# A row transform of 512 points as four products of 128 columns, with first-layer weights loaded in rearranged quarters

## The chip, the cores and the metric

One core of one Trainium2 chip runs the kernel. Its engines work side by side: TensorE (PE) multiplies matrices, VectorE (DVE) and ScalarE (ACT) work element by element, GpSimd (POOL) does small work and issues DMAs, SyncE (SP) only issues DMAs. The time is that of one execution on the device in microseconds (us); the median of several runs is what counts.

## The reference

The input x has 2048 rows of 512 numbers, in bf16. Each row is normalized (xn), and three terms are added:

```python
xn = _layernorm(x, axis=-1)
return x + _A_ref(xn, A_w_r, A_w_i) + _B_ref(xn, B_w_gate, B_w_up, B_w_down)

def _A_ref(x, w_r, w_i):       # S = 2048, D = 512, weights [2048, 257]
    X = rfft2(x.astype(float32), axes=(-2, -1))
    return irfft2(X * (w_r + 1j * w_i), s=(S, D)).astype(bfloat16)

def _B_ref(x, w_gate, w_up, w_down):    # 512 -> 1792 -> 512
    g, u = x @ w_gate, x @ w_up
    return (gelu(g) * u) @ w_down
```

So there is a two-dimensional Fourier filter over all rows (A) and a gated feed-forward layer (B), both on the same normalized rows.

## The kernel before

**Tiles.** The 2048 rows are 16 tiles j of 128 rows; four tiles make a block m. For each tile DVE takes statistics (`ln_stat`, `ln_aggr`; for tiles 0 and 1 `ln_first`, with ACT's square root), GpSimd raises the variance to the power -1/2 (L683, all tiles but 0 and 1), and `ln_norm` writes the normalized row in one operation of 512 columns, on DVE (12 tiles) or ACT (4). `trans` turns the tile with four PE transpositions (it needs the identity, `ident`), and DVE or ACT copy the result from PSUM to `xnT[m]`: four chunks `dc` of 128 of the 512 columns on the partitions, 512 rows along the free axis.

**Feed-forward.** `gate_up` (L990) multiplies weight chunks with `xnT`, for each block and each of 14 blocks `fc` of 128 hidden columns. The first four `fc` of block 0 are done in two parts, tiles 0 and 1 first, then 2 and 3. Blocks 2 and 3 use a scheme with seven products (`gate_up7`, L1074). `down` (L1168) is the second layer, also with seven products; its last product in the last block is `last_prod` (L1183), two halves of 256 columns in two PSUM banks, each followed by an add on DVE (L1188); two output DMAs wait for both adds.

**Filter.** `butter` folds the 512 columns of a block: chunks 0, 1 plus and minus chunks 2, 3 (two operations of 1024 columns, L740 and L741), and the sum once more (two of 512, L742 and L743). `unit_D` (L754 to L757) is the transform along a row, 16 units: the frequencies divisible by 4 and those 2 off that have one product of 128 columns each, while the odd ones have two products of 256 columns over 2 x 128 rows of weights. ACT brings the result to `xs`. Then come `unit_A` and a trip through DRAM (`scr1`, back into `tv`), `unit_B`, the filter, `unit_C`, a second trip, `unit_E` and `unit_F`. `unit_B` needs all eight pieces of `tv`.

**Loads.** Each of the two weight matrices of the first layer is loaded in five pieces by `load_w`: ten DMAs on SP, each over all 128 partitions and all four chunks `dc`, 256 KB for two `fc`. x comes in halves of 64 partitions, the first ones by SP and ACT; the row transform's constants `fd` in one DMA of 192 KB.

**Order.** A list scheduler (`_Plan`) runs while the kernel is built. It gives every instruction a fixed place in its engine's queue, by assumed durations and a priority for each of 1026 tasks, written out in `ORDER`; `GATES` holds some late DMAs and DVE steps back until PE has come to a given priority. [...] SP's start list before is 26 DMAs; GpSimd's queue begins with two memsets, then the powers of tiles 2 and 3, then those of later blocks and the late DMAs (L670: the second layer's weights, the filter's weights `W`, constants).

Of the kernel before, what the change touches and what calls it, by code (L numbers as in the profile page):

```python
# [29 lines left out]
def _constants():  # L30
# [9 lines left out]
    m64 = np.arange(64)[None, :]  # L40
    a0 = tp * (p + 0.5) * (4 * m64) / D
    a2 = tp * (p + 0.5) * (4 * m64 + 2) / D
    im0 = -np.sin(a0)
    im0[:, 0] = (-1.0) ** np.arange(P)
    fo = []
    for c in range(2):
        kodd = np.concatenate([4 * m64[0] + 1, 4 * m64[0] + 3])[None, :]
        a = tp * (p + P * c + 0.5) * kodd / D
        fo += [np.cos(a), -np.sin(a)]
    FD = np.concatenate([np.cos(a0), im0, np.cos(a2), -np.sin(a2)] + fo, 1)  # L50
# [426 lines left out]
def bass_parallel_sum__spectral_gfnet__glu_gated_geglu__prompt_kernel(  # L477
# [25 lines left out]
    with ExitStack() as es:  # L503
# [103 lines left out]
        def act(fn, n, r, w, prio, over=(), **kw):  # L607
            return add("act", fn, r=r, w=w, over=over, occ=n / 1200 + 0.055, lat=n / 1200 + 0.24, prio=prio, **kw)
# [13 lines left out]
        def wkey(nm, fs, dcs=(0, 1)):  # L622
            return [("w" + nm, f, i) for f in fs for i in dcs]
# [821 lines left out]
```

## Time and profile before

| | us |
|---|---|
| runs shown | 176.8, 178.35, 178.53; median 178.35 |
| profiled execution | 176.34 |
| its span (first to last instruction) | 174.5 |
| PE, DVE, ACT, POOL busy | 169.8, 150.4, 118.4, 51.2 |
| mean granted clock of PE | 0.999 |

Busy time is the union of an engine's instructions, and matmuls overlap: one of 256 columns is shown with 0.273 us, while the next starts 0.107 to 0.11 after it. "Idle before" in a group is the engine's idle time ahead of its instructions, and the releaser is what ended it. The 1.84 us between span and execution lie outside the profile's instructions.

### The profile page before, as it was taken

The numbers are of one execution on the slowest core, as the hardware profiler recorded it, in microseconds if no ns is written. First come the engines' busy times: TensorE is split into PE (matmuls) and PEld (weight loads), VectorE is DVE, ScalarE is ACT, GpSimd is POOL, SyncE is SP. The second block draws the span as 40 slices with busy tenths as digits, with TensorE's granted clock in tenths as the row PEclk, the third lists the DMA queues.
The fourth block names the chain that finished last, engine by engine and source line by source line (L and its number), as shares of the span: only waits on it lengthen the run. The fifth ranks groups of instructions, "written<-read, shape, count | busy, mean of one in ns | idle before, by whom it ended". The sixth has DMA issues, their size and how long they took to land.

```text
span 174.5 us, 4179 instructions
## 1 busy us (share of the span) xinstructions
PE 169.8 (97%) x1594; PEld 124.8 (71%) x1594; DVE 150.4 (86%) x346; ACT 118.4 (68%) x209; POOL 51.2 (29%) x88
## 2 busy tenths in 40 slices
PE   7999999999999999999999999999999999999992
PEld 2577655547767764444778877889999989888881
DVE  2689899988898434999997899999999999998992
ACT  3434885998855224468563879979979999987200
POOL 2020240557975958557881210000000000000000
PEclk9999999999999999999999999999999999999999
DMA  2999999599997999725799354500002543000013
GB/s 73 243 291 269 246 296 273 143 326 212 274 171 187 265 260 163 124 59 154 181 244 287 91 154 119 125 0 4 4 0 64 120 110 74 0 0 4 0 30 90
DMA packets 21811, 25.00 MB, mean 143 GB/s; under 512 B 3264, under 2 KB 17984, under 8 KB 21536
## 3 DMA queue, kind: packets, MB, share of 16 engines
q1 hardware_dynamic: 18144, 17.21, 38.9%
q0 software_dynamic: 3056, 7.21, 17.1%
q10 hardware_dynamic: 592, 0.33, 0.7%
q8 instruction: 12, 0.20, 0.5%
q14 instruction: 7, 0.06, 0.1%
HBM read 18.44 MB, written 6.29 MB: 142 GB/s over the span
## 4 chain that ended last, share of the span: by engine, by line
PE 96%; DVE 2%; issue 0%; DVEq 0%
PE ps L990 27%; PE ps L1074 25%; PE ps L1168 24%; PE ps L1266 4%; PE ps L883 2%; PE ps L714 2%; PE ps L934 2%; PE ps L912 2%; PE ps L862 1%; PE ps L774 1%; PE ps L757 1%; PE ps L777 1%; PE ps L756 1%; PE ps L1183 1%; DVE st L674 1%; PE ps L755 1%
## 5 line engine op out<-in xcount | busy, mean ns | idle before, releaser
L990 PE MATMUL ps<-xw,wg 128*128 128x512 f16 (+2 forms) x144 | 28.1, 332 | 0.0
L997 ACT ACTIVATE gl<-ps 128x512 bf16<-128x512 f32 (+1 forms) x32 | 17.0, 552 | 16.2 <-PE ps L990 12.0
L990 PE MATMUL ps<-xw,wu 128*128 128x512 f16 (+1 forms) x128 | 27.1, 353 | 0.0
L990 PEld LDWEIGHTS ps<-xw,wu 128*128 128x128 bf16 x128 | 11.9, 98 | 11.3 <-DMA wu<-in_B_w_up_dram 0.5
L670 POOL DMA_DIRECT2D xw<-in_A_w_r_dram x28 | 16.5, 599 | 9.2 <-PE ps L1074 4.5
L990 PEld LDWEIGHTS ps<-xw,wg 128*128 128x128 bf16 x144 | 12.2, 98 | 9.6 <-issue 0.6
L1003 DVE TENSOR_TENSOR hT<-ps,gl 128x512 bf16<-128x512 f32 (+1 forms) x26 | 15.0, 600 | 4.3 <-ACT gl L997 3.1
L670 POOL DMA_DIRECT2D xw<-in_A_w_i_dram x28 | 16.2, 590 | 4.9 <-PE ps L1168 2.7
L1087 ACT ACTIVATE gl<-ps 128x512 bf16<-128x512 f32 x28 | 16.0, 598 | 0.8 <-PE ps L1074 0.6
L1074 PE MATMUL ps<-xw,wg 128*128 128x256 f16 x112 | 16.2, 273 | 0.0
L1074 PE MATMUL ps<-xn,wu 128*128 128x256 f16 x112 | 15.7, 273 | 0.0
L1074 PE MATMUL ps<-xn,ws 128*128 128x256 f16 x112 | 15.7, 273 | 0.0
L1168 PE MATMUL ps<-wd,hT 128*128 128x256 bf16 x112 | 13.6, 273 | 0.0
L1168 PE MATMUL ps<-wdt,hs 128*128 128x256 f16 x112 | 13.4, 273 | 0.0
L1168 PE MATMUL ps<-wd,hs 128*128 128x256 bf16 (+1 forms) x112 | 13.2, 273 | 0.0
L867 ACT ACTIVATE bc<-ps 128x1024 f16<-128x1024 f32 x8 | 8.2, 1023 | 6.9 <-PE ps L862 4.0
L674 DVE BATCH_NORM_STATS2 st<-x_sb 128x6 f32<-128x512 bf16 x16 | 10.5, 680 | 2.4 <-DMA x_sb<-in_A_x_dram 2.1
L1168 PEld LDWEIGHTS ps<-wdt,hs 128*128 128x128 f16 x112 | 10.7, 98 | 1.8 <-DVE wdt L1136 0.4
L1168 PEld LDWEIGHTS ps<-wd,hT 128*128 128x128 bf16 x112 | 10.7, 98 | 1.8 <-issue 0.2
L1074 PEld LDWEIGHTS ps<-xw,wg 128*128 128x128 bf16 x112 | 10.4, 98 | 1.9 <-issue 0.4
L1074 PEld LDWEIGHTS ps<-xn,wu 128*128 128x128 f16 (+1 forms) x112 | 10.5, 98 | 1.8 <-issue 0.2
L1168 PEld LDWEIGHTS ps<-wd,hs 128*128 128x128 f16 x112 | 10.8, 98 | 1.4 <-DVE x_sb L1203 0.2
(132 smaller groups left out, 370.4 us busy)
## 6 DMA issues: line engine op xcount, KB each, us to landing
scr<-ta SPq DMA_DIRECT2D x32, 64.0 KB, 5.3
tv<-scr SPq DMA_DIRECT2D x8, 256.0 KB, 5.0
scr<-bc SPq DMA_DIRECT2D x16, 128.0 KB, 2.5
area<-scr SPq DMA_DIRECT2D x8, 256.0 KB, 3.8
xw<-in_A_w_r_dram POOLq DMA_DIRECT2D x28, 64.0 KB, 4.0
xw<-in_A_w_i_dram POOLq DMA_DIRECT2D x28, 64.0 KB, 4.1
x_sb<-in_A_x_dram SPq DMA_DIRECT2D x6, 256.0 KB, 9.3
out_dram<-x_sb SPq DMA_DIRECT2D x12, 128.0 KB, 2.3
```

The source lines that it names most:

```text
L670: add("pool", lambda e: e.dma_start(dst, src), r=r, w=w, over=over, occ=0.7, lat=kb / 1024 / 0.27, prio=prio, gate=prio, dma=True)
L674: add("dve", lambda e: e.bn_stats(st[:, j, :], x_sb[:, j, :]), r=[("x", j, 0), ("x", j, 1)] + behind, w=[("st", j)], occ=0.6, lat=0.75, pr ...
L714: ins = e.transpose(bank_h(v)[:, i * P:(i + 1) * P], xn[:, jj, dc * P:(dc + 1) * P], ident[:])
L867: act(lambda e: e.activation(xc.rearrange("p k h c -> p (k h c)"), pair(v), ACT.Copy, scale=SC_B), 1024, [("ps", v)], [("xc",)], prio + K[ ...
L883: ins = e.matmul(bank(v, hh)[64 * kl:64 * kl + 64, 256 * z:256 * z + 256], cm[64 * hh:64 * hh + 64, 2 * H + z, kl, 32 - 32 * i:96 - 32 * i ...
L990: ins = e.matmul(bank(v)[:, w * i:w * i + w], w_sb[nm][:, dc, fc * P:(fc + 1) * P], xnT[m][:, dc, c0 + w * i:c0 + w * i + w], start=(dc == ...
L997: act(lambda e: e.activation(gl[k][:, 0:n], bank(vs[0])[:, 0:n], ACT.Gelu_apprx_tanh), n, [("ps", v)], [("gl", k)], prio)
L1003: dve(lambda e: e.tensor_tensor(o, bank(vs[1])[:, 0:n], gl[k][:, 0:n], ALU.mult), n, [("ps", vs[1]), ("gl", k)], ks, prio + K["dH"])
L1074: ins = e.matmul(bank(v)[:, 256 * q:256 * q + 256], W_, B0[:, dc, :], start=(first and q == 0 and dc == 0), stop=(dc == 1), skip_group_che ...
L1087: act(lambda e: e.activation(gl[k][:], bank(v), ACT.Gelu_apprx_tanh), 512, [("ps", v)], [("gl", k)], prio + K["aG"])
L1168: ins = e.matmul(bank(v)[:, 256 * t:256 * t + 256], A0[:, f, P * t:P * t + P], B0[:, f, :], start=(first and t == 0 and f == 0), stop=(f = ...
L1266: ins = e.matmul(bank(v), dumm[:, 0:128], dumm[:, 0:512], start=True, stop=True)
```

## The change

- **Fold.** Both halves of the first fold are folded again: four operations of 512 columns instead of two. For the odd frequencies that needs point n beside point 255 - n, so the columns are put in another order on the partitions: in even chunks `dc` the two halves of 64 are swapped, in odd chunks each half of 64 runs backwards.
- **Row transform.** `unit_D` is four products of 128 columns with four 128 x 128 constants; `fd` shrinks from 768 to 512 columns (128 KB). ACT's eviction to `xs` now reads in order and writes every second element.
- **Norm.** `ln_norm` writes that order in two operations of 256 columns (even chunks, odd chunks).
- **Weights.** The rows of the gate and up weights must have the same order. `load_w` is four DMAs instead of one: SP loads the two swapped halves of the even chunks, 64 partitions each; GpSimd loads the odd chunks, one DMA for each, with rows running backwards in groups of 64 ("falling quarters"). That makes 20 DMAs on SP and 20 on GpSimd for ten on SP.
- **Last product.** `last_prod` has three parts, 256, 128 and 128 columns, in three PSUM banks with three adds.
- **Queues.** `ident` is loaded by ACT, by ORDER after its first table load. On ACT the halves of tiles 1 and 0 change places. GpSimd's memsets move: by the new `ORDER` eight weight pieces (blocks 0 to 3) come first, then the memset of `nn`, two more pieces, `mhalf`, one more, and only then the powers of tiles 2 and 3. SP's start list has 35 DMAs.
- **Order.** `ORDER` has 1082 entries, all new, and `GATES` is new. The scheduler's assumed durations for DMAs change. The second block's units and all later ones of the row transform move among the products; the last `unit_A` comes later among the down products of block 0 and the gate and up products of block 1.

```diff
-    m64 = np.arange(64)[None, :]
-    a0 = tp * (p + 0.5) * (4 * m64) / D
-    a2 = tp * (p + 0.5) * (4 * m64 + 2) / D
-    im0 = -np.sin(a0)
+    r = np.arange(P)[:, None] ^ 64
+    ae, ao = tp * (r + 0.5) * 2 * m / D, tp * (r + 0.5) * (2 * m + 1) / D
+    im0 = -np.sin(ae)
...
-    fo = []
-    for c in range(2):
-        kodd = np.concatenate([4 * m64[0] + 1, 4 * m64[0] + 3])[None, :]
-        a = tp * (p + P * c + 0.5) * kodd / D
-        fo += [np.cos(a), -np.sin(a)]
-    FD = np.concatenate([np.cos(a0), im0, np.cos(a2), -np.sin(a2)] + fo, 1)
+    FD = np.concatenate([np.cos(ae), im0, np.cos(ao), -np.sin(ao)], 1)
...
-                        begin = max(now + occ + 0.8, rings[e])
+                        begin = max(now + occ + 0.3, rings[e])
...
-                        t.done = rings[e] + (2.2 if now < 18 else 2.6)
+                        t.done = rings[e] + (2.1 if now < 18 else 3.1)
...
-        tmp = area[:, 0:1024].rearrange("p (a c) -> p a c", a=2)
+        tmp = [area[:, 1024 * i:1024 * i + 1024].rearrange("p (a c) -> p a c", a=2) for i in range(2)]
...
-        def wkey(nm, fs, dcs=(0, 1)):
+        def wkey(nm, fs, dcs=(0, 1, 2, 3)):
...
-        def load_w(nm, lo, hi, eng, prio, dcs=(0, 1)):
...
-            src = (B_w_gate if nm == "g" else B_w_up).rearrange("(dc p) f -> p dc f", p=P)
+        def load_w(nm, lo, hi, prio, eng="sp"):
...
+            src = (B_w_gate if nm == "g" else B_w_up).rearrange("(dc i p) f -> i p dc f", i=2, p=P)
...
-            ds = slice(2 * dcs[0], 2 * dcs[-1] + 2)
-            dma(eng, w_sb[nm][:, ds, cs], src[:, ds, cs], w=wkey(nm, range(lo, hi), dcs), prio=prio, kb=64 * len(dcs) * (hi - lo))
+            n = hi - lo
+            for a in range(2):
+                dma(eng, w_sb[nm][64 * a:64 * a + 64, ::2, cs], src[0][64 - 64 * a:128 - 64 * a, :, cs], w=wkey(nm, range(lo, hi), (a,)), prio=prio + 0.01 * a, kb=32 * n)
+            for i in range(2):
+                v = src[1][:, i, cs].rearrange("(a q) f -> a q f", a=2)[:, ::-1]
+                add("pool", lambda e, v=v, i=i: e.dma_start(w_sb[nm][:, 2 * i + 1, cs], v), w=wkey(nm, range(lo, hi), (2 + i,)), occ=0.85,
+                    lat=32 * n / 1024 / 0.24, prio=prio + 0.02 + 0.01 * i, dma=True)
...
-        add("pool", lambda e: e.memset(mhalf[:], -0.5), w=[("mhalf",)], occ=0.1, lat=0.3, prio=-100)
-        add("pool", lambda e: e.memset(nn, 0.0), w=[("nz",)], occ=1.0, lat=1.2, prio=-99)
...
-        dma("sp", ident[:], c_id.ap(), w=[("ident",)], prio=-99.2, kb=32)
-        load_w("g", 0, 2, "sp", -99)
-        load_x(2, 2, 0, "sp", -98.5)
-        load_x(2, 2, 1, "sp", -98)
-        load_w("u", 0, 2, "sp", -97.5)
-        load_w("g", 2, 4, "sp", -97)
-        load_w("u", 2, 4, "sp", -96.5)
-        load_w("g", 4, 8, "sp", -96)
-        load_w("u", 4, 8, "sp", -95)
+        dma("act", ident[:], c_id.ap(), w=[("ident",)], prio=-99.2, kb=32)
+        load_w("g", 0, 2, -99)
+        add("pool", lambda e: e.memset(mhalf[:], -0.5), w=[("mhalf",)], occ=0.1, lat=0.3, prio=-98.7)
+        load_w("u", 0, 2, -98.5)
+        load_x(2, 2, 0, "sp", -98)
+        load_x(2, 2, 1, "sp", -97.5)
+        load_w("g", 2, 4, -97)
+        load_w("u", 2, 4, -96.5)
+        load_w("g", 4, 8, -96)
+        load_w("u", 4, 8, -95)
...
 ...
-        dma("sp", fd[:], c_fd.ap(), w=[("fd",)], prio=-93, kb=192)
+        add("pool", lambda e: e.memset(nn, 0.0), w=[("nz",)], occ=1.0, lat=1.2, prio=-94)
+        dma("sp", fd[:, 0:512], c_fd.ap(), w=[("fd",)], prio=-93, kb=128)
...
-        load_w("g", 8, 11, "sp", -92)
-        load_w("u", 8, 11, "sp", -91)
+        load_w("g", 8, 11, -92)
+        load_w("u", 8, 11, -91)
...
-        load_w("g", 11, 14, "sp", -88)
-        load_w("u", 11, 14, "sp", -87)
+        load_w("g", 11, 14, -88)
+        load_w("u", 11, 14, -87)
...
         def ln_norm(j, prio, eng="dve"):
-            if eng == "act":
-                act(lambda e: e.activation(xn[:, j % 4, :], x_sb[:, j, :], ACT.Identity, bias=nmr[:, j:j + 1], scale=rstd[:, j:j + 1]), 770,
-                    [("x", j, 0), ("x", j, 1), ("nmr", j), ("rstd", j)], [("xn", j % 4)], prio)
-                return
-            add("dve", lambda e: e.tensor_scalar(xn[:, j % 4, :], x_sb[:, j, :], ag[:, j, 0:1], rstd[:, j:j + 1], ALU.subtract, ALU.mult),
-                r=[("x", j, 0), ("x", j, 1), ("ag", j), ("rstd", j)], w=[("xn", j % 4)], occ=0.33, lat=0.47, prio=prio)
...
+            xq = x_sb[:, j, :].rearrange("p (d i a c) -> p i d a c", i=2, a=2, c=64)
+            o = xn[:, j % 4, :].rearrange("p (d i a c) -> p i d a c", i=2, a=2, c=64)
+            for i, (xi, oi) in enumerate(((xq[:, 0], o[:, 0][:, :, ::-1]), (xq[:, 1], o[:, 1][:, :, :, ::-1]))):
+                if eng == "act":
+                    act(lambda e, xi=xi, oi=oi: e.activation(oi, xi, ACT.Identity, bias=nmr[:, j:j + 1], scale=rstd[:, j:j + 1]), 500,
+                        [("x", j, 0), ("x", j, 1), ("nmr", j), ("rstd", j)], [("xn", j % 4, i)], prio)
+                else:
+                    add("dve", lambda e, xi=xi, oi=oi: e.tensor_scalar(oi, xi, ag[:, j, 0:1], rstd[:, j:j + 1], ALU.subtract, ALU.mult),
+                        r=[("x", j, 0), ("x", j, 1), ("ag", j), ("rstd", j)], w=[("xn", j % 4, i)], occ=0.2, lat=0.33, prio=prio)
 ...
-            dve(lambda e: e.tensor_tensor(tmp, x[:, 0:2, :], x[:, 2:4, :], ALU.add), 1024, xk(m), [("tmp",)], prio, x=2)
-            dve(lambda e: e.tensor_tensor(f[:, 2:4, :], x[:, 0:2, :], x[:, 2:4, :], ALU.subtract), 1024, xk(m), [k + (1,)], prio, x=2)
-            dve(lambda e: e.tensor_tensor(f[:, 0, :], tmp[:, 0], tmp[:, 1], ALU.add), 512, [("tmp",)], [k + (0,)], prio, x=2)
-            dve(lambda e: e.tensor_tensor(f[:, 1, :], tmp[:, 0], tmp[:, 1], ALU.subtract), 512, [("tmp",)], [k + (2,)], prio, x=2)
+            t, d = tmp[0], tmp[1]
+            dve(lambda e: e.tensor_tensor(t, x[:, 0:2, :], x[:, 2:4, :], ALU.add), 1024, xk(m), [("tmp", 0)], prio, x=2)
+            dve(lambda e: e.tensor_tensor(d, x[:, 0:2, :], x[:, 2:4, :], ALU.subtract), 1024, xk(m), [("tmp", 1)], prio, x=2)
+            for i, (s, op) in enumerate(((t, ALU.add), (t, ALU.subtract), (d, ALU.subtract), (d, ALU.add))):
+                dve(lambda e, i=i, s=s, op=op: e.tensor_tensor(f[:, i, :], s[:, 0], s[:, 1], op), 512, [("tmp", i // 2)], [k + (i,)], prio, x=2)
         def unit_D(j, prio):
...
             def fn(e):
-                o = bank(v).rearrange("p (a r c) -> p a r c", a=2, r=4)
-                e.matmul(o[:, :, 0, :], f[:, 0, c], fd[:, 0:128], start=True, stop=False, skip_group_check=True)
-                e.matmul(o[:, :, 2, :], f[:, 1, c], fd[:, 128:256], start=False, stop=False, skip_group_check=True)
-                e.matmul(o[:, :, 1::2, :], f[:, 2, c], fd[:, 256:512], start=False, stop=False, skip_group_check=True)
-                return e.matmul(o[:, :, 1::2, :], f[:, 3, c], fd[:, 512:768], start=False, stop=True, skip_group_check=True)
-            pe(fn, [P, P, 256, 256], [("fd",)] + [k + (i,) for i in range(3)], [("ps", v)], prio, alloc=(v, 1, False), full=True)
+                ins = None
+                for i in range(4):
+                    ins = e.matmul(bank(v)[:, P * i:P * i + P], f[:, i, c], fd[:, P * i:P * i + P], start=(i == 0), stop=(i == 3), skip_group_check=True)
+                return ins
+            pe(fn, [P] * 4, [("fd",)] + [k + (i,) for i in range(4)], [("ps", v)], prio, alloc=(v, 1, False), full=True)
...
-            act(lambda e: e.activation(x4.rearrange("p (a c r) -> p a c r", a=2, r=4),
-                                       bank(v).rearrange("p (a r c) -> p a c r", a=2, r=4), ACT.Copy, scale=SC_D),
+            act(lambda e: e.activation(x4.rearrange("p (a c r) -> p r a c", a=2, r=2),
+                                       bank(v).rearrange("p (r a c) -> p r a c", a=2, r=2), ACT.Copy, scale=SC_D),
...
 ...
            def last_prod(p):
...
-                for t in range(2):
+                for i, (t, c0, c1) in enumerate(((0, 0, 256), (1, 0, 128), (1, 128, 256))):
...
-                    def fn(e, t=t, v=v):
+                    n = c1 - c0
...
+                    def fn(e, t=t, v=v, c0=c0, c1=c1):
...
-                            ins = e.matmul(bank(v)[:, 0:256], A0[:, f, P * t:P * t + P], B0[:, f, :], start=(f == 0), stop=(f == 6))
+                            ins = e.matmul(bank(v)[:, 0:c1 - c0], A0[:, f, P * t:P * t + P], B0[:, f, c0:c1], start=(f == 0), stop=(f == 6))
...
-                    pe(fn, [256] * 7, ka(0, 7) + kb, [("ps", v)], p + 0.1 * t, main=True, alloc=(v, 1, False))
+                    pe(fn, [n] * 7, ka(0, 7) + kb, [("ps", v)], p + 0.1 * i, main=True, alloc=(v, 1, False))
...
-                    xo = x_sb[:, j, 0:256]
-                    dve(lambda e, t=t, xo=xo, v=v: e.tensor_tensor(xo, bank(v)[:, 0:256], mu[2][:, 256 * t:256 * t + 256], ALU.add), 256,
-                        [("ps", v), ("mu", 2)], [("xe", t)], p, over=[("xa", t1, 0)])
+                    xo = x_sb[:, j, c0:c1]
+                    dve(lambda e, t=t, xo=xo, v=v, c0=c0, n=n: e.tensor_tensor(xo, bank(v)[:, 0:n], mu[2][:, 256 * t + c0:256 * t + c0 + n], ALU.add), n,
+                        [("ps", v), ("mu", 2)], [("xe", i)], p, over=[("xa", t1, 0)])
...
-                        r=[("xe", 0), ("xe", 1)], w=[("out", t1, b, 0)], prio=p + 0.2)
+                        r=[("xe", i) for i in range(3)], w=[("out", t1, b, 2)], prio=p + 0.2, kb=64)
```

More of the change, by code (lines that the diff above doesn't have):

```diff
@@ L339, in refill @@
             b = c[-1]
-            t.i, t.eng, t.fn, t.r, t.w, t.over = len(T), "pe", (lambda e: self.fill(e, b)), (("wg", 0, 0), ("wg", 0, 1)), (("bank", b),), ()
+            t.i, t.eng, t.fn, t.r, t.w, t.over = len(T), "pe", (lambda e: self.fill(e, b)), (("wg", 0, 0), ("wg", 0, 1), ("wg", 0, 2), ("wg", 0, 3)), (("bank", b),), ()
             t.occ, t.lat, t.prio, t.dma, t.mode, t.alloc, t.res, t.full = 0.216, 0.216, 0.0, False, "m", None, 0, True
@@ L715, in f @@
                 return ins
-            pe(f, [P] * (len(dcs) * len(jjs)), [("ident",)] + [("xn", jj) for jj in jjs], [("ps", v), ("tr", m, dcs, jjs)], prio, alloc=(v, 1, False))
+            pe(f, [P] * (len(dcs) * len(jjs)), [("ident",)] + [("xn", jj, i) for jj in jjs for i in range(2)], [("ps", v), ("tr", m, dcs, jjs)], prio, alloc=(v, 1, False))
             w = len(jjs) * P
```

14 lines of the change are left out of this document (7 added, 7 removed), and 103 rows, old and new, of tables (GATES, ORDER).

## The prediction

> **What bounds the kernel now.** I read the page's busy rows first, then its slices, then the chain that ended last, then busy time by stretch.
>
> ```profile
> PE 169.8 (97%) x1594; PEld 124.8 (71%) x1594; DVE 150.4 (86%) x346; ACT 118.4 (68%) x209; POOL 51.2 (29%) x88
> PE   7999999999999999999999999999999999999992
> PEclk9999999999999999999999999999999999999999
> PE 96%; DVE 2%; issue 0%; DVEq 0%
> 12.00:50.00 38.00, 37.96 (x315) 23.63 (x314) 34.86 (x92) 30.39 (x52) 17.21 (x25) 1.00 0.99 250
> ```
>
> TensorE (PE) is busy in every slice but the first and the last, at full granted clock, and the chain is 96% PE. The last line is the stretch 12 to 50 us (PE, PEld, DVE, ACT, POOL, then clock, DMA share, GB/s): PE has no gap, DVE has 3.1 us free in 38, and the DMA engines are full. So a microsecond of matmul taken away is a microsecond of the whole, as long as nothing else is late for PE's fixed order. From 0 to 12 us PE is mostly warming up on zeros (13 matmuls, 5.73 us), and the chain there runs through the norm of the first rows. After PE stops come the last add, two output DMAs and the end.
>
> The profiled execution took 176.34 us, a span of 174.5 and 1.84 around it; the median shown, 178.35, is 2.01 above it. I work out a difference against the profiled execution and apply it to the median.
>
> **1. The products of the transform (removed: columns).** One unit of four matmuls, in the timeline of PE (start, duration):
>
> ```profile
> 16.82 0.22 PE L754 MATMUL ps<-fd,area 128*128 128x128 f16 x1
> 16.87 0.22 PE L755 MATMUL ps<-fd,area 128*128 128x128 f16 x1
> 16.93 0.27 PE L756 MATMUL ps<-fd,area 128*128 128x256 f16 x1
> 17.04 0.27 PE L757 MATMUL ps<-fd,area 128*128 128x256 f16 x1
> 17.14 0.22 PE L754 MATMUL ps<-fd,area 128*128 128x128 f16 x1
> ```
>
> Matmuls overlap, so a cost is the distance of starts, not the duration: 128 columns take 0.055, 256 take 0.107, a unit 0.32. Four of 128 columns take 0.22: 0.105 saved, 16 units, **-1.7 us**. That 128 columns with a weight load each keep this pace is seen at L754 itself and at L912, eight such in 0.45 (chain, 118.09). All 16 units lie where PE has no gap.
>
> **2. The tail.** Timeline of the end:
>
> ```profile
> 169.49 1.69 PE L1183 MATMUL ps<-wdt,hT 128*128 128x256 f16 x14
> 170.56 0.42 DVE L1188 TENSOR_TENSOR x_sb<-ps,ac 128x256 bf16<-128x256 f32 x1
> 171.22 0.42 DVE L1188 TENSOR_TENSOR x_sb<-ps,ac 128x256 bf16<-128x256 f32 x1 [0.24 <-PE ps L1183]
> ```
>
> The last add waits for PE and is then alone. Now PE's second half is two products of seven matmuls of 128 columns, 14 x 0.055 = 0.77 for 7 x 0.109 = 0.76: nothing. The last add has 128 columns: PSUM adds take 0.684 for 512 and 0.42 for 256, so about 0.29. **-0.13 us.** The middle add starts 0.39 before the last product ends and is done in time.
>
> **3. Weights in four pieces (10 DMAs become 20 on SP and 20 on GpSimd).** SP's early issues take 0.44 to 0.76 each. By the new ORDER the second SP piece of gate 0-2 is SP's fifth issue, about 3.4 us instead of 2.90; both SP pieces of up 0-2 end near 6.3 instead of 5.7. A DMA of 64 KB on 64 partitions lands in 2.4 to 2.7 us (x_sb), one of 256 KB in 4.1, so gate 0-2 lands near 6.1 to 7.0, under the warm-up as before (first use 7.8); up 0-2 lands at 8.4 to 9.2 where PE wants it at about 8.6. Identity moves behind ACT's table load, issued near 3.5 and landing 2.1 later, 5.6 to 6.2, with PE on zeros until 6.95: covered by 0.8. So is the swapped order of the first x halves on ACT (0.6 later). Cost 0 to 0.6, taken **+0.2**. [...]
>
> Later, the DMA engines are full to 24 us and a transfer issued at 10 to 16 us lands 10 us later (gate and up 384 KB, 10.8 and 10.3). SP's start list grows from 26 to 35 issues; the last pieces of blocks 8 to 13 now stand 29th to 35th, 17 to 22 us, and ORDER moves the gate product of block 12 up, from 32.9: five products of 0.86, a pair of transpositions (0.9) and four transform units (1.3) now come after it, one product before it, so it comes near 27. [...] Below zero it cannot go, since PE had no gap to give back. 0 to +1.0, taken **+0.3**.
>
> **4. Norm halves and the GpSimd queue (added: a wait).** Rows 2 and 3 get their scale from a power on GpSimd:
>
> ```profile
> 9.42 0.15 DVE L681 TENSOR_SCALAR vpe<-ag 128x1 f32<-128x1 f32 x1
> 9.65 0.57 POOL L683 TENSOR_TENSOR rstd<-vpe,mhalf 128x1 f32<-128x1 f32 x1 [7.93 <-DVE vpe L681]
> 10.43 0.38 DVE L703 TENSOR_SCALAR xn<-x_sb,ag,rstd 128x512 f16<-128x512 bf16 x1
> ```
>
> GpSimd sat idle 7.93 us before. Now 11 DMA issues and two memsets (0.95, 0.10) stand ahead of that power, and the second power, both norms, four transposes and the second half of the first block hang on it. An issue costs:
>
> ```profile
> L670 POOL DMA_DIRECT2D xw<-in_A_w_r_dram x28 | 16.5, 599 | 9.2 <-PE ps L1074 4.5 <-PE ps L990 2.9 <-PE ps L1168 1.0
> L670 POOL DMA_DIRECT2D wd<-in_B_w_down_dram x4 | 3.1, 774 | 7.2 <-PE ps L990 7.2
> L670 POOL DMA_DIRECT2D wn<-in_A_w_r_dram x1 | 1.1, 1102 | 0.0
> ```
>
> The new pieces are 64 to 128 KB in rows of 512 to 1024 B, like the first of these rows: 0.60, free at 0.74 + 11 x 0.60 + 1.05 = 8.4, before 9.57. No row runs backwards through DRAM, so the ends are 0.55 and 1.10. The norm itself: 404 ns for 512 columns; DVE's 16-bit operations go from 417 (512) to 686 (1024), 0.525 a column, so a half is 270 and two cost +0.14; reversed outputs are no dearer (L944 writes backwards, 414, as L943). Two norms in turn: +0.2 to 0.3 before the transposes of row 3. Between lie gate and up products of rows 0 and 1, 3.5 us of PE, so part is hidden. 0.1 to 3.5, taken at 0.60 an issue: **+0.3**.
>
> **5. DVE.** Two more 512-column operations in each of four butterflies, 0.35 apart at this size (14.16 to 14.51), 2.8 us; twelve norms by 0.14, 1.7; together 4.5 against 3.1 free in 12 to 50. ACT's four halved norms add about 0.4 each (828 ns, 0.85 a column), with 7.6 free. DVE can push statistics of the last rows past 50, where it has 8.8 of 24 free, as ORDER does; but it also frees PSUM banks. 0 to +1.4 (the excess on PE), taken **+0.3**.
>
> **6. Round trip through DRAM.** ORDER moves the last blocks' transform back among the products: between the last unit_A and the first unit_B stand twelve gate or up products of 0.86 and two of 1.53 on the way down, 14 us with the small ones, where the trace has 19.3 (54.6 to 73.9). The trip takes about 0.1 + 1.02 (eviction) + 1.8 (four issues) + 5.3 (scr) + 5.0 (tv) = 13.3: covered by 0.7; with the longest landing of tv, 8.6 for 5.0, late by 2.9. 0 to 2.9, taken **0**, since medians fit.
>
> **Sum:** -1.7 - 0.13 + 0.2 + 0.3 + 0.3 + 0.3 = -0.7, so 175.6 for the profiled execution and **177.6** for the median. 1% (1.8 us) is about what a measurement of this kernel can tell from no change.
>
> **Rivals.** *All covers hold*: terms 3 to 5 vanish, -1.83, 176.5. For it: PE had no gap, early DMA engines and GpSimd were idle. Against: DVE's 3.1 us. Chance 0.17. *GpSimd's issues are dear* (slower). At d us an issue the power starts at 1.8 + 11 d and row 2's transposes 1.36 later (1.22 in the trace, and 0.14); PE runs out of rows 0 and 1 near 11.5, so it idles 11 d - 8.35: from 0.76 it costs, from 0.93 it eats the whole gain, and at wn's 1.08 it is 3.5: 176.34 - 1.83 + 3.5 = 178.0, median 180.0; late pieces of gate 0-2 (fourth on that queue) come on top. Chance 0.2. [...] *DVE or the DRAM trip becomes the bound*: 1.1 more from term 5 makes 178.7, a tv late by 1.2 as well 179.9. For it: DVE's 4.5 against 3.1; against: the 8.8 free after 50. Chance 0.18. *The matmuls get no cheaper* (weight loads, 98 ns, show): refuted by L754 and L912, 0.02. The forecast, -1.4 to -0.2, has 0.43.
>
> **Range.** From 176.2 (all gain, a little measurement) to 180.3 (GpSimd at 1.08 and a late piece). Faster by over 1% is only the full gain: 0.17. Slower by over 1% is the GpSimd case and the upper end of the third: 0.22. Within 1%: 0.61.
>
> **What would show it.** Starts of the four products 0.055 apart (term 1); a last add near 0.29 (2); PE's gaps between 8 and 13 us, and who ended them (3, 4); the mean of the weight issues on POOL, 0.60 or near 1; the power's start at 9.7 or later; gaps near 27 us ended by wg or wu DMAs; DVE's busy time from 12 to 50; PE waiting for tv near 74. I am wrong if PE shows more than 2 us of new gaps, or if PE's order puts in extra fill matmuls.

## The result and the profile after

The changed kernel takes **194.8 us** (median of 194.01, 193.04, 195.62 and 195.63), the kernel before 177.7 beside it: a ratio of 1.100, 95% interval 1.094 to 1.106. The forecast was 177.6, from 176.2 to 180.3; the kernel is 17 us slower, far outside. Every ratio below is against the kernel before as it ran beside that kernel (medians 176.5 to 177.7); a run that fell into a slower state of the chip counts in a median but not in a ratio.

From the page of the changed kernel (busy row, slices of 4.8 us, packets, chain):

```profile
span 193.8 us, 4269 instructions
PE 176.2 (91%) x1601; PEld 127.2 (66%) x1601; DVE 156.1 (81%) x367; ACT 121.8 (63%) x213; POOL 66.9 (35%) x108
PE   7629763799999999999999999999999999999993
PEclk9955978589999999999999999999999999999999
DMA  3999999975796857597457994442000246000013
GB/s 88 151 128 182 210 175 181 173 143 138 194 327 144 205 143 203 134 287 141 113 129 197 238 247 139 136 108 60 2 3 0 58 108 150 16 0 3 0 27 83
DMA packets 23188, 25.02 MB, mean 129 GB/s; under 512 B 6768, under 2 KB 18928, under 8 KB 22912
PE 73%; DVE 12%; DMA 4%; issue 4%; SPq 3%; ACT 2%; POOL 1%; DVEq 0%; ACTq 0%
```

Before, PE was at 9 in every slice but the first and the last; now seven of the first eight show 2 to 7 tenths, and its granted clock falls to one half in three of the eight. From the ninth slice on PE is full again. The DMA row says 9 tenths in that stretch, but look at the row below it. The same rows of the kernel before, with its packets:

```profile
DMA  2999999599997999725799354500002543000013
GB/s 73 243 291 269 246 296 273 143 326 212 274 171 187 265 260 163 124 59 154 181 244 287 91 154 119 125 0 4 4 0 64 120 110 74 0 0 4 0 30 90
DMA packets 21811, 25.00 MB, mean 143 GB/s; under 512 B 3264, under 2 KB 17984, under 8 KB 21536
```

In that stretch the DMA engines show the same 9 tenths and move 128 to 210 GB/s instead of 243 to 296. By stretch, first the kernel before, then the changed one (PE, PEld, DVE, ACT, POOL, clock, DMA share, GB/s):

```profile
12.00:24.00 12.00, 11.97 (x105) 7.91 (x104) 10.95 (x30) 8.25 (x17) 1.02 (x1) 1.00 1.07 273
24.00:36.00 12.00, 11.99 (x95) 6.92 (x95) 11.58 (x36) 9.80 (x18) 4.80 (x7) 1.00 0.88 232
```

```profile
12.00:24.00 12.00, 9.40 (x75) 7.10 (x72) 6.59 (x19) 2.31 (x7) 6.34 (x9) 0.68 1.12 185
24.00:36.00 12.00, 5.63 (x30) 3.42 (x31) 4.23 (x15) 4.14 (x8) 2.97 (x4) 0.75 1.14 175
```

And the start in the changed kernel's timeline of PE (in brackets PE's idle time, and what ended it):

```profile
8.92 0.40 PE L721 MATMUL ps<-ident,xn 128*128 128x128 f16 x4 [0.15 <-DVE xn L710]
11.64 1.44 PE L997 MATMUL ps<-xw,wg 128*128 128x128 f16 x12 [2.32 <-DMA wg<-in_B_w_gate_dram]
14.91 1.89 PE L997 MATMUL ps<-xw,wu 128*128 128x256 f16 x8 [1.83 <-DMA wu<-in_B_w_up_dram]
21.60 1.04 PE L997 MATMUL ps<-xw,wu 128*128 128x256 f16 x8
```

The first gate product begins at 11.64 (before 7.83), the first up product at 14.91 (before 8.85); both wait for a weight DMA. The last two lines are eight matmuls of one shape, 1.89 us and 1.04; the granted clock was 0.50 from 14.90 to 16.80 us and 1.00 from 21.60 to 22.60. So PE, which had waited 1.83 us for these weights, lost a second time here, 0.85 us in eight matmuls.

To compare kernels I use one sum, worked out from the traces' starts, **PE's gaps**: for each matmul, the distance to the start of the next above what its columns take on a fed PE (0.056 us for 128, 0.109 for 256, 0.216 for 512), where that is over 0.03 us. The warm-up is in it (2.5 us before), and so is time lost to a lower clock.

```
PE's gaps, us        0-12  12-24  24-36  36-50  50-62  62-end   sum   last matmul ends
kernel before         3.4    0.4    0.3    0.3    0.2    2.2    6.8        171.2
changed kernel        6.9    7.8    6.8    2.2    0.7    3.5   27.9        190.6
```

21.1 us more gaps, less 1.6 of matmul columns, is 19.5; the last matmul ends 19.4 later (these two executions took 176.34 and 195.62). So the ledger closes: the columns were saved, and all of the loss is waiting and low clock.

### The profile page after: what moved, and what is told of

Read it like the earlier page. It is cut to its first block, busy times and chain, and to the rows that moved or that the text cites. A ratio compares the mean times of both kernels' runs of the same rounds, so it can differ in the third digit from the quotient of the medians.

```text
span 193.8 us, 4269 instructions
## 1 busy us (share of the span) xinstructions
PE 176.2 (91%) x1601; PEld 127.2 (66%) x1601; DVE 156.1 (81%) x367; ACT 121.8 (63%) x213; POOL 66.9 (35%) x108
## 2 busy tenths in 40 slices
DMA packets 23188, 25.02 MB, mean 129 GB/s; under 512 B 6768, under 2 KB 18928, under 8 KB 22912
## 4 chain that ended last, share of the span: by engine, by line
PE 73%; DVE 12%; DMA 4%; issue 4%; SPq 3%; ACT 2%; POOL 1%; DVEq 0%; ACTq 0%
PE ps L1081 22%; PE ps L1175 21%; PE ps L997 18%; DMA wu<-in_B_w_up_dram 4%; SPq L612 3%; PE ps L890 2%; DVE st L677 2%; DVE xn L710 2%; PE ps L941 2%; PE ps L919 2%; PE ps L763 2%; DVE hT L1010 1%; DVE hs L1164 1%; DVE area L751 1%; ACT gl L1004 1%
## 5 line engine op out<-in xcount | busy, mean ns | idle before, releaser
L997 PE MATMUL ps<-xw,wu 128*128 128x512 f16 (+1 forms) x128 | 31.6, 395 | 6.4 <-issue 4.6
L997 PE MATMUL ps<-xw,wg 128*128 128x512 f16 (+2 forms) x144 | 30.0, 354 | 4.9 <-DMA wg<-in_B_w_gate_dram 2.3
L997 PEld LDWEIGHTS ps<-xw,wu 128*128 128x128 bf16 x128 | 13.1, 110 | 18.9 <-issue 7.5
L997 PEld LDWEIGHTS ps<-xw,wg 128*128 128x128 bf16 x144 | 13.7, 108 | 16.5 <-issue 5.4
L767 ACT ACTIVATE area<-ps 128x512 f16<-128x512 f32 x16 | 10.9, 754 | 4.3 <-PE ps L763 4.1
L1081 PEld LDWEIGHTS ps<-xw,wg 128*128 128x128 bf16 x112 | 10.4, 98 | 2.0 <-issue 0.4
L1081 PEld LDWEIGHTS ps<-xn,ws 128*128 128x128 f16 x112 | 10.7, 98 | 1.6 <-issue 0.2
## 6 DMA issues: line engine op xcount, KB each, us to landing
x_sb<-in_A_x_dram SPq DMA_DIRECT2D x6, 256.0 KB, 17.4
```

The costliest lines, as they stand in the source:

```text
L767: act(lambda e: e.activation(x4.rearrange("p (a c r) -> p r a c", a=2, r=2), bank(v).rearrange("p (r a c) -> p r a c", a=2, r=2), ACT.Copy ...
L997: ins = e.matmul(bank(v)[:, w * i:w * i + w], w_sb[nm][:, dc, fc * P:(fc + 1) * P], xnT[m][:, dc, c0 + w * i:c0 + w * i + w], start=(dc == ...
L1081: ins = e.matmul(bank(v)[:, 256 * q:256 * q + 256], W_, B0[:, dc, :], start=(first and q == 0 and dc == 0), stop=(dc == 1), skip_group_che ...
```

## Experiments

Two things changed together in the start, the loads and the row transform with its norm. The first batch parts them.

**The loads alone, in the kernel before** (`load_w` as in the changed kernel; fold, norm and last product as before):

```diff
-            dma(eng, w_sb[nm][:, ds, cs], src[:, ds, cs], ...)
+            for a in range(2):
+                dma(eng, w_sb[nm][64 * a:64 * a + 64, ::2, cs], src[0][64 - 64 * a:128 - 64 * a, :, cs], ...)
+            for i in range(2):
+                v = src[1][:, i, cs].rearrange("(a q) f -> a q f", a=2)[:, ::-1]
+                add("pool", lambda e, v=v, i=i: e.dma_start(w_sb[nm][:, 2 * i + 1, cs], v), ...)
```

> The kernel before (old fold, old norm, last product in two banks) with the changed kernel's loads of the first weights alone: two 64-partition pieces by SP and two falling pieces by GpSimd for each load (the weights' rows then stand in another order than the old fold's, so the product is another one). Theory 'loads' (falling rows or pieces): the whole loss is here, 192 to 197. Rival 'fold': the loss comes from norm halves, eviction or order; then 177 to 180.

198.85 us, ratio 1.123 (1.115 to 1.131), above the 192 to 197 of its theory. **The loads are the loss**, and somewhat more than all of it.

**All but the loads** (the changed kernel with one SP transfer per load, as before):

```diff
-            for a in range(2): dma(eng, w_sb[nm][64 * a:64 * a + 64, ::2, cs], ...)
-            for i in range(2): add("pool", ... e.dma_start(w_sb[nm][:, 2 * i + 1, cs], v) ...)
+            dma(eng, w_sb[nm][:, :, cs], src[:, :, cs], ...)
```

> The changed kernel with the first weights loaded in one SP transfer each, as before: the finer fold, the norm in halves, the strided eviction, the ident on ACT, and the three banks alone (rows of the weights not permuted, so the product is another one). By my terms 1 and 2 less the norm and DVE terms 4 and 5 it would be 176.0 to 178.5, the best 176.5. Theory 'loads': 176 to 178.5. Rival 'fold': above 185.

180.09 us, ratio 1.018 (1.004 to 1.031). The 15 us are gone, but it is above the 176.0 to 178.5 that I expected: a second, smaller loss, taken up below.

**Which property of the loads?** The changed kernel with the quarters rising in one run of 128 rows:

```diff
-                v = src[1][:, i, cs].rearrange("(a q) f -> a q f", a=2)[:, ::-1]
+                v = src[1][:, i, cs]
```

> The changed kernel with one thing other: GpSimd's two pieces of each load read their 128 rows rising in one run instead of each 64 rows falling; as many pieces, bytes and issues on the same queues, in the same order on every engine (the rows of the odd chunks then stand in another order than the transform expects, so the product computed is another one). Theory 'falling rows': the 3024 records of 16, 24 and 32 bytes, absent before, which only the falling pieces bring, slow all queues; without them the 64 KB pieces land in 2.5 to 4 us again, the first gate product starts before 9 us, and the time is 176 to 180. Rival 'pieces': four transfers for one, of which two reach 64 partitions alone, slow the loads whichever way the rows run; the time stays at 193 to 196 and SP's 512-byte records at 60 to 90 ns. Rival 'fold': the loads are only late because of the rest; 193 to 196 too.

180.19 us, ratio 1.019 (1.011 to 1.027), 0.2 over the range and level with one transfer per load. The 40 pieces in place of 10, two of each four on 64 partitions, cost nothing that can be measured in the whole. At the start they do cost: the first up product begins at 10.78 us, with one transfer per load at 9.65, and PE's gaps up to 12 us are 5.3 against 3.5; later gaps are smaller, and the sums are 12.3 and 11.5. Then falling rows in 16 groups of 8, not 2 groups of 64:

```diff
+                v = src[1][:, i, cs].rearrange("(g r) f -> g r f", r=8)[:, ::-1]
```

> The changed kernel with GpSimd's pieces falling within groups of 8 rows, the 16 groups of a piece rising, instead of falling within 2 groups of 64; bytes, issues and order of work as in the changed kernel (the odd chunks' rows again stand in another order, so the product is another one). If it is the falling step itself (from one row to the one below it), 7 of 8 steps still fall: 190 to 196, with the small records still there. If it is that the outermost dimension of the falling pieces counts 2, so that few of the engines share a piece, 16 groups mend it: 176 to 180. If it is the number of pieces: 193 to 196.

181.51 us, ratio 1.028 (1.016 to 1.040), 1.5 over the 176 to 180 of a mended load. Seven of eight steps still fall, and 13 of the 15 us are gone. So **falling is not it**; my theory that the loss came with the falling step fell here. The opposite, 2 groups of 64 rows that rise:

```diff
+                v = src[1][64 * i:64 * i + 64, :, cs].rearrange("q d f -> d q f")
```

> The changed kernel with GpSimd's pieces as 2 groups of 64 rising rows (64 rows of one odd chunk, then the same 64 of the other) instead of 2 groups of 64 falling ones; bytes, issues and order stay (the rows stand in another order, so the product is another one). Theory 'two groups' (a piece whose outermost dimension counts 2 is shared out badly): 190 to 197, with the records of 16 to 32 bytes in the software queue. Rival 'long fall' (64 rows falling in one run are what is slow, 8 are not): 179 to 182, without them.

195.15 us, ratio 1.104 (1.097 to 1.112): the whole loss, without one falling row. What the two slow kernels share, and the two with 180.19 and 181.51 have not, is a source whose outermost dimension has two entries. Two kernels between, 4 groups of 32 and 8 of 16, tell whether the time follows the count or two groups are a special case:

> The changed kernel with GpSimd's pieces as 4 groups of 32 falling rows (the groups rising; the rows stand in another order, so the product is another one). If a piece goes to as many of the 16 engines as its outermost dimension counts: with 2 groups a 64 KB piece took 1.7 to 1.9 us of SP's queue where the falling quarters were SP's, about 37 GB/s or an eighth of the 296 GB/s at best; 4 groups would have a quarter, the 1.83 MB of the quarters 25 us on 4 engines beside some 20 us for the rest: late loads still, 184 to 191. If only the pattern of two times 64 is bad: 180 to 183.

> The changed kernel with GpSimd's pieces as 8 groups of 16 falling rows (the rows again in another order). If a piece goes to as many engines as its outermost dimension counts: half of them, 12 us for the quarters beside some 20 us for the rest, about what 16 groups need in all: 181 to 184. If only two times 64 is bad: 180 to 182.

188.25 us (1.065, 1.057 to 1.073) and 183.77 (1.040, 1.032 to 1.047), each inside the range that sharing by count gave. In one table, with rows of the pages (a 64 KB piece of the gate weights from GpSimd, median us from issue to landing; mean GpSimd time of an issue of gate pieces; packets under 512 B in all):

```
groups of rows in a piece      us      landing   issue   packets < 512 B
1 x 128 rising               180.19      3.4      0.55        3744
16 x 8 falling               181.51      3.3      0.61        3744
8 x 16 falling               183.77      4.4      0.65        4192
4 x 32 falling               188.25      5.3      0.70        5088
2 x 64 falling (changed)     194.81      7.9      0.84        6768
2 x 64 rising                195.15      7.8      0.86        6769
```

From the view of DMA issues, the changed kernel and then the kernel with rising quarters (KB of one, median us to landing):

```profile
x_sb<-in_A_x_dram SPq DMA_DIRECT2D x6, 256.0 KB, 17.4
wg<-in_B_w_gate_dram POOLq DMA_DIRECT2D x4, 64.0 KB, 7.9
wg<-in_B_w_gate_dram SPq DMA_DIRECT2D x4, 64.0 KB, 7.5
```

```profile
x_sb<-in_A_x_dram SPq DMA_DIRECT2D x6, 256.0 KB, 7.7
wg<-in_B_w_gate_dram POOLq DMA_DIRECT2D x4, 64.0 KB, 3.4
wg<-in_B_w_gate_dram SPq DMA_DIRECT2D x4, 64.0 KB, 3.9
```

Not only the pieces with two groups are late. SP's pieces of the same weights and the rows of x, which nobody touched, take twice as long. In the trace's records SP's packets of 512 B took 84 ns in the mean between 8 and 14 us of the changed kernel, 29 with rising quarters, and 31 in the kernel before.

The trace also has each step of the semaphore that tells of a load's landing, 16 steps for each of these loads. For the first gate piece from GpSimd, in us after the start of its issue:

```
1 x 128 rising             sixteen from 2.12 to 3.02
16 x 8 falling             sixteen from 2.00 to 2.97
8 x 16 falling             sixteen from 2.07 to 3.10
4 x 32 falling             twelve from 2.25 to 2.91, four from 3.84 to 4.01
2 x 64 falling (changed)   fourteen from 2.77 to 3.15, then 5.34 and 5.56
2 x 64 rising              fourteen from 2.58 to 3.35, then 5.78 and 6.24
```

As many steps are late as the piece has groups, for two and for four, as if the bytes were shared by that many of 16 engines. For eight the steps do not part.

**Is it GpSimd's queue?** The changed kernel with the falling quarters issued by SP:

```diff
-                add("pool", lambda e, v=v, i=i: e.dma_start(w_sb[nm][:, 2 * i + 1, cs], v), ...)
+                add("sp", lambda e, v=v, i=i: e.dma_start(w_sb[nm][:, 2 * i + 1, cs], v), ...)
```

> The changed kernel, whole, with the falling quarters issued by SP instead of GpSimd (the order of all engines follows, since the planner sees SP's queue longer by 20 issues). If two outermost groups are badly shared out on any queue: 190 to 200. If only the software queue does it badly: 180 to 185, the 20 issues of about 0.6 us that SP has more, less what hides them, on top of the 180 of the rising pieces.

221.49 us, ratio 1.253 (1.244 to 1.261): worse than either theory had it (190 to 200, or 180 to 185). Its page shows the cause barer than the changed kernel's (slices of 5.5 us):

```profile
PE   7159558641498899999799999999988997999993
DMA  2225524242669984456932699624100044400013
GB/s 83 87 85 147 134 89 127 75 139 79 160 178 257 249 218 121 135 152 176 199 105 66 170 224 285 172 74 112 49 4 0 3 96 96 99 0 0 3 24 72
```

In the first ten slices the DMA engines are 2 to 5 tenths busy, while PE waits for weights (7.7 us at once for a gate piece) and SP's issues stall (two from 4.71 us on take 2.26, one from 21.30 takes 3.20, the shortest 0.53). Each falling piece of 64 KB held up the landings behind it by about 1.7 us, together with the 64 KB that landed next; at 296 GB/s, the best of the first seven slices before, that neighbour is worth 0.22, so the piece ran at 64 KB in 1.5 us, 44 GB/s or 0.15 of the 296. The profile counts 16 engines; two of them would be 0.125. So I estimate that about two engines carried each falling quarter, as many as it has groups. The times with 4 and 8 groups, 188.25 and 183.77 us, lie in the ranges (184 to 191, 181 to 184) worked out from that estimate, and the late steps above, two with two groups and four with four, agree with it. That the engines follow the count of groups is inferred from these numbers alone.

On SP's queue the count shows more directly. Each of the 20 falling quarters shows three steps in place of 16: one 0.94 to 1.29 us after the start of its issue, and two when it lands, at 4.03 us or later. Each of the 34 loads of weights, x and constants that SP issued after the first of them has 16, and in 31 of them the longest wait between steps is that before the last two: 1.69 us in the median, with the fold alone 0.14. That is how two engines of 16 would look that carry all the quarters, with every other load waiting for its share of these two. In the changed kernel the late steps of SP's loads are more: its second 64 KB gate piece had ten steps by 3.93 us and six from 5.79 to 7.09. That the quarters hold the same two engines each time on SP's queue and various ones on GpSimd's would explain 221 against 195. The records name no engine, so both are argued, not shown.

One rival is left, packets of 16, 24 and 32 bytes (3024 in the changed kernel): the fewer the groups, the more packets under 512 B GpSimd's queue carries (last section). With SP issuing there are none of these, and 3464 packets under 512 B in all, and yet the loss is larger. So they are not the cause.

**The second loss.** In the kernel with the fold alone, what PE waited for in longer waits:

```profile
PE ps L1274 <- DVE epst L635: 1.2, 1, 1.2
PE ps L780 <- ACT area L766: 0.6, 1, 0.6
PE ps L720 <- DVE xn L709: 0.5, 1, 0.5
PE ps L762 <- DVE area L750: 0.5, 1, 0.5
PE ps L996 <- DVE hT L1009: 0.3, 1, 0.3
```

Past the warm-up (first line) the next three are the transform's eviction (area by ACT), the norm (xn) and the fold (area by DVE): the work that the finer fold made dearer. Their rows in the first 62 us, first before and then with the fold alone:

```profile
L703 DVE TENSOR_SCALAR xn<-x_sb,ag,rstd 128x512 f16<-128x512 bf16 x12 | 4.6, 404 | 0.5 <-POOL rstd L683 0.4
L743 DVE TENSOR_TENSOR area<-area 128x512 f16<-128x512 f16 x4 | 1.7, 419 | 0.0
L742 DVE TENSOR_TENSOR area<-area 128x512 f16<-128x512 f16 x4 | 1.7, 417 | 0.0
L760 ACT ACTIVATE area<-ps 128x512 f16<-128x512 f32 x16 | 8.6, 616 | 3.1 <-PE ps L757 3.1
```

```profile
L709 DVE TENSOR_SCALAR xn<-x_sb,ag,rstd 128x256 f16<-128x256 bf16 x24 | 7.3, 337 | 0.6 <-POOL rstd L685 0.5
L750 DVE TENSOR_TENSOR area<-area 128x512 f16<-128x512 f16 x16 | 5.8, 413 | 0.0
L766 ACT ACTIVATE area<-ps 128x512 f16<-128x512 f32 x16 | 10.5, 755 | 0.7 <-PE ps L762 0.7
```

DVE does 2.7 us more of norms and 2.4 more of folding; ACT's eviction, which now writes every second element, takes 755 ns for 616. I took that work away in place, with every other instruction where it stood in the plan:

```diff
-            for i, (xi, oi) in enumerate(((xq[:, 0], o[:, 0][:, :, ::-1]), (xq[:, 1], o[:, 1][:, :, :, ::-1]))):
+            for i, (xi, oi) in enumerate(((x_sb[:, j, :], xn[:, j % 4, :]), (None, None))):   # the second is left out
-            dve(lambda e: e.tensor_tensor(d, x[:, 0:2, :], x[:, 2:4, :], ALU.subtract), ...)
+            dve(lambda e: e.tensor_tensor(f[:, 2:4, :], x[:, 0:2, :], x[:, 2:4, :], ALU.subtract), ...)   # and the last two folds left out
-            act(lambda e: e.activation(x4.rearrange("p (a c r) -> p r a c", a=2, r=2), bank(v).rearrange(...), ...))
+            act(lambda e: e.activation(x4, bank(v), ...))
```

> The kernel with the fold alone (first weights in one rising transfer each), with the VectorE and ScalarE work that the finer fold adds taken away again and every instruction else in its place in the order: the norm in one instruction a tile, the last two of the six fold operations left out (their columns come from one subtraction, so the odd half of the transform is another one), the eviction of the transform plain instead of interleaved (columns then stand in another order). VectorE loses 2.7 + 2.4 us and ScalarE 1.4 + 2.2 us of work. Theory 'load': the 2.4 us over the kernel before are VectorE and ScalarE having too little room between 12 and 60 us; the time falls to 175.5 to 177.5, under the kernel before by the 1.7 us of matmul columns. Rival 'order': the due times of the changed kernel cost it, whatever the engines have to do; it stays at 179 to 181.

The norm alone and the eviction alone:

> The kernel with the fold alone, and the norm of a tile in one plain instruction instead of two reversed halves (the columns of the odd chunks are then not reversed, so the transform is another one). VectorE's 24 halves of 337 ns become 12 of about 404 in the first 62 us (busy 7.3 to 4.6 us), ScalarE's 8 of 590 become 4 of 828. Theory 'load', by the norm: 178 to 179, over half of the loss. If the fold operations or the eviction carry it: 179.5 to 180.5. Rival 'order': 179.5 to 180.5.

> The kernel with the fold alone, and ScalarE's eviction of the transform plain (columns then in another order) instead of interleaved by two: 16 of about 616 ns instead of 755, 2.2 us of ScalarE. Theory 'load', by ScalarE: 178.5 to 179.3. If VectorE carries the loss alone: 179.8 to 180.5. Rival 'order': 179.5 to 180.5.

All three: 178.07 us, ratio 1.008 (1.004 to 1.011). The norm alone: 178.71, 1.011 (1.007 to 1.014). The eviction alone: 179.79, 1.016 (1.011 to 1.021), no measurable difference from the 1.018 of the fold. 1.018 less 1.008 would be 1.8 us for the added work, but the interval of the fold alone, 1.004 to 1.031, holds both. The same work taken away under two other sets of due times (below) moved the ratio from 1.052 to 1.044 and from 1.043 to 1.029, some 1.5 and 2.4 us, the second clear of its intervals. So the added work costs about 2 us; that most of it is the norm in two instructions is what the medians suggest, not shown. Theory "load" expected 175.5 to 177.5, under the kernel before, and rival "order" 179 to 181; the time lies between them: it is 1.3 us over the kernel before, with 1.6 us less for PE to do. Nearly 3 us of waiting are left, and its trace has 2.7 us more gaps:

```
PE's gaps, us          0-12  12-24  24-36  36-50  50-62  62-end   sum
kernel before           3.4    0.4    0.3    0.3    0.2    2.2    6.8
fold alone              3.5    2.4    0.1    1.5    1.6    2.4   11.5
  norm whole            3.6    1.4    0.4    0.4    1.9    2.2    9.9
  all three taken away  3.8    1.5    0.1    0.3    1.2    2.5    9.4
  + old due times       3.4    0.8    0.0    1.2    1.1    9.0   15.4
  + mixed due times     2.8    0.8    0.1    2.6    0.5    6.8   13.5
```

Of the 2.7 us, 1.1 lie at 12 to 24 (the transposes of tiles 2 and 3 wait for their norm) and 1.0 at 50 to 62 (the last transform). I suspected the new due times, and gave the tasks those of the kernel before:

```diff
-ORDER = [... of the changed kernel ...]
+ORDER = [... of the kernel before; a task split in two has those of its whole ...]
```

> The kernel with the fold alone and the added VectorE and ScalarE work taken away (as j_all_three: norm in one instruction, two fold operations left out, plain eviction), and with the due times of the kernel before for every task instead of the changed kernel's (a task that is split in two takes those of its whole). Theory 'load and order': what is left of the loss in j_all_three, some 3 us against the 1.7 us that its transform saves, is the order; here the transposes of tiles 2 and 3 wait no longer, and the time is 174 to 176, under the kernel before. Rival 'something else in the fold' (the four matmuls wait for four operands, the ident on ACT): 177 to 179 as j_all_three.

> The kernel with the fold alone, all its VectorE and ScalarE work kept, and the due times of the kernel before. Theory 'load and order' with both halves alike: 176.5 to 178.5, under the 180 of the fold with the changed kernel's due times and over the same order without the load. Rival 'order is made for the load' (the due times of the changed kernel fit the added work, the old ones don't): 179.5 to 182.

184.30 us (1.044, 1.039 to 1.049) and 186.43 (1.052, 1.047 to 1.058): worse than with the new due times. The gap table shows that order matters all the same: up to 36 us the old due times do close the gaps (4.2 us, about as before), and after 62 us they open new ones, 9.0. So I kept the old ones for the tasks due in the first 36 us alone:

> The kernel of j_all_three (fold alone, added VectorE and ScalarE work taken away) with the due times of the kernel before for the tasks that were due there in the first 36 us, and the changed kernel's for all later ones. With the old due times throughout, PE's gaps up to 36 us were 4.2 us (the kernel before 4.0, j_all_three 5.4), and what it lost came after 62 us. Theory 'early order': the 1.2 us come back, 176 to 177.5, level with the kernel before. Rival 'no order to blame, each order has its own gaps': 177.5 to 180.

> The kernel with the fold alone and all its added work, and the same mixed due times. Theory 'early order': 1.2 us less than the 180.1 of the changed kernel's due times, 178.3 to 179.5. Rival 'each order has its own gaps': 179.5 to 182.

182.53 (1.029, 1.023 to 1.035) and 184.17 (1.043, 1.038 to 1.047), above every range expected. Again the early gaps close (3.7 us up to 36) and later ones open. The theories of order failed as I had put them: no set of due times that I tried gives the transform's 1.6 us back. That the rest sits in the order of the work, and not in a resource, is argued from where the gaps move, not shown by a kernel without them; whether an order exists that has neither stays open. No kernel of the study beats the kernel before.

## Why the prediction was wrong, step by step

**Step 3, the weights in four pieces, failed.** It priced a piece by its size and its partitions ("a DMA of 64 KB on 64 partitions lands in 2.4 to 2.7 us") and the later ones at 0 to 1.0, taken +0.3. For splitting as such that was right in the whole: 180.19 against 180.09. But the falling quarters have a shape that no transfer of the trace had, two groups of rows outermost, and I bounded their issue on GpSimd ("no row runs backwards through DRAM, so the ends are 0.55 and 1.10") and never their landing. That unbounded term, in a step taken at 0.5 us in all, was 14.6 us (194.81 less 180.19): the first quarter's semaphore had its last two steps 2.2 us after the rest, from which I estimate that two of 16 engines carried it, and the loads beside the quarters were late too (x rows 17.4 us, with rising quarters 7.7). I looked at the new feature that caught the eye, the backward run, and it cost next to nothing (181.51 against 180.19, intervals that overlap); the plain count of two beside it cost everything. The nearest rival had pieces that come late because GpSimd issues them late; none had pieces that are slow once issued.

In the whole the runs show no cost of the pieces on 64 partitions, 180.19 us against 180.09, though the intervals (1.011 to 1.027 and 1.004 to 1.031) would hide one of a few tenths of a us; whether the first up product, 10.78 us for 9.65, is late by the halves or by the number of pieces no run tells apart.

**Step 4, GpSimd's queue: issue dearer than taken, but not what was waited for.** An issue took 0.84 us (wg; 0.82 wu) instead of 0.60, between my break-even of 0.76 and the 0.93 that would eat the gain:

```profile
L632 POOL DMA_DIRECT2D wg<-in_B_w_gate_dram x10 | 8.2, 841 | 0.8 <-POOLq L1439 0.8
12.94 0.58 POOL L686 TENSOR_TENSOR rstd<-vpe,mhalf 128x1 f32<-128x1 f32 x1 [1.89 <-DVE vpe L684]
```

Yet the power of tile 2, at 12.94, came after 1.89 us of idle GpSimd: it waited for DVE, and DVE's statistics of that tile, at 11.75, had waited 1.97 us for x. The queue was not the limit there. With rising quarters an issue was 0.55, with two rising groups 0.86: the price came with the groups. So the slower rival named the right place and the wrong mechanism.

**Step 5, DVE: right in size, wrong in price.** I forecast 4.5 us more DVE work and the pages show 4.4 (154.8 with the fold alone, 150.4 before), but less in the folding and more in the norm: a half took 337 ns, not 270, so two cost 0.27 more than the whole, not 0.14. The price was +0.3 (0 to 1.4), with +0.3 more for the norm in step 4; taking the work away, with ACT's, won about 2 (1.5 and 2.4 in two pairs). I had not listed ACT's eviction (0.14 us each, 16 times) in the sum; alone it costs nothing measurable.

**Step 1, the columns: right.** From the chain of the changed kernel in order of time (start, us), 16 matmuls of four units at full clock:

```profile
63.88 1.05 PE ps L763 x16
```

Starts lie 0.056 apart, so a unit takes 0.22 instead of 0.33; 16 units, 1.7 us. **Step 2, the tail**: from the start of the last product to the end of the span 5.01 us before, 4.94 with the fold alone and 4.96 in the changed kernel: -0.05 to -0.07 for -0.13, in the noise either way. **Step 6, the trip through DRAM: right.** With the fold alone, the last `unit_A` ends its issue at 63.3, the last piece of `tv` lands at 77.0 and `unit_B` starts at 77.3; PE does not wait. The 14 us forecast between the two units was 14.0.

**What was missing altogether.** The sum took 1.7 us of shorter matmuls as a microsecond for a microsecond. With the loads mended and the added DVE and ACT work gone, 2.7 us of gaps remained, more than the gain. My "I am wrong if PE shows more than 2 us of new gaps" was the right alarm: there were 21.

## What to carry to other kernels

Ahead of sizes and partitions, read the outermost dimension of a DMA's source: here 64 KB from a source that starts with a dimension of 2 landed in 7.9 us, from one run of 128 rows in 3.4, and the x rows beside it in 17.4 for 7.7. A transfer in a shape that the trace does not hold has no bound from its neighbours in size; put its landing, not only its issue, among the unknowns. And work taken from a PE without a gap is not yet time: here 1.6 us less of matmuls, with more work for DVE and ACT, gave a ratio of 1.018, and 1.008 with that work gone. Price the engines that feed PE in the same stretch.

## What the runs showed of the hardware

- Time against the groups of a piece: 195.2 us for 2, 188.3 for 4, 183.8 for 8, 181.5 for 16, and 180.2 for one run of 128 rows. I had not expected that 1.83 MB of 25 could do this.
- GpSimd's issue time follows the groups as well, 0.55 us for 1 x 128 to 0.86 for 2 x 64, and with few groups the software queue carries small packets that are not there otherwise: 3024 with two groups (6768 less 3744 in the table; 16, 24 and 32 bytes in the changed kernel), 1344 with four, 448 with eight, none with sixteen, and none with SP issuing. What they are the trace does not say.
- The pieces whose source starts with a dimension of two landed in a pattern of their own: on SP's queue the semaphore showed three steps in place of 16; on GpSimd's, the first gate piece had fourteen by 3.15 us and two at 5.34 and 5.56. The loads behind them on SP's queue waited 1.69 us (median of 31) for their last two steps.
- The DMA share did not follow the bytes moved. With GpSimd issuing, the page showed 9 tenths and 128 to 210 GB/s, before 9 tenths and 243 to 296; with SP issuing the same pieces, 2 to 5 tenths and 75 to 147 in the first ten slices. Read GB/s beside the share.
- PE's granted clock fell to 0.68 in the mean from 12 to 24 us when PE was 78% busy, and eight matmuls of one shape took 1.89 us for 1.04. Before, the clock was 1.00 there, with PE busy for 11.97 of the 12 us.
